# Attention decode, one core: keys loaded in rows of 64 KB instead of 32 KB, in a ring where two units overlap by half

## The chip, the cores and the metric

One core of one Trainium2 chip. Times are device microseconds (us) of that core, median of several executions. 1 KB is 1024 bytes where rows and loads are meant. A "packet" is what the trace records for one row of a load on one of the core's 16 transfer engines (DMA engines).

## The reference, cut to what matters

One token for each of 4 batches goes through attention over a cache of 8192 keys and values, and then through a gated layer. The caches are 256 MiB each in bf16, and each byte is used once.

```python
B, Sq, D = 4, 1, 512
H, Sk, Dh = 32, 8192, 128
q = (layernorm(x) @ wq).reshape(B, Sq, H, Dh).transpose(0, 2, 1, 3)
scores = einsum("bhqd,bhkd->bhqk", q, k_cache) * Dh ** -0.5
o = einsum("bhqk,bhkd->bhqd", softmax(scores), v_cache)
h = x + o.transpose(0, 2, 1, 3).reshape(B, Sq, H * Dh) @ wo
out = h + (sigmoid(ln(h) @ w_gate) * (ln(h) @ w_up)) @ w_down
```

## The kernel before

A *unit* is four heads of one batch: 8 MiB of keys and 8 MiB of values; there are 32. In SBUF a unit is 128 partitions of 64 KB, and partition p holds 256 consecutive positions of one head, so in memory too each partition's row is 64 KB in one piece.

A unit is worked off in 4 *steps* of 16 KB per partition. A step's keys are transposed by DVE (4 instructions), and PE computes their scores (16 matmuls). 8 steps, two units, make a *group*, after which comes one softmax. The values follow with 64 matmuls a unit ("PV").

The ring has four slots of 32 KB per partition. Values take a row of 64 KB (slots 2 and 3). Keys take two loads of 32 KB rows, one to slot 0, one to slot 1, and each slot is filled again as soon as its two steps are transposed.

```python
GS = 8            # steps in a group
NS = 4            # slots in the ring
LB = 16           # steps in a turn of the loops of PE and DVE
TW = R * 64       # elements of a slot: 32 KB per partition
HT = TW // 2      # elements of a step: 16 KB per partition
ring = SB("ring", [128, NS, TW], BF16)
kT = SB("kT", [128, 2, HT], BF16)              # transposed keys, two steps
bS, bO, bP = bank[0:2], bank[2:4], bank[4:6]   # PSUM: two score banks, two output banks

items = [("wq", 0)]
for u in range(NU):
    items += [("k", 2 * u), ("k", 2 * u + 1)]
    ...                                        # and the values of unit u - 1

# what a load waits for
prev_of[it] = [("k", it[1] - 2)]               # keys: the slot's last keys transposed
prev_of[it] = [("pv", it[1] - 1)]              # values: PV of the unit before
# ... [cut: first and last units]

def load(it):
    ...
    if kind == "k":
        dst, src = ringv(t % 2), kv_src(t // 2, A_k_cache)[:, (t % 2) * TW:(t % 2 + 1) * TW]
    elif kind == "v":
        dst, src = ringf[:, v_at(t, w0):...], kv_src(t, A_v_cache)[:, w0 * HT:w1 * HT]
    return [(lambda e: e.dma_start(dst, src).then_inc(sem, 16), sem, val)]

for s in range(NST):                           # 128 steps
    g, at = divmod(s, GS)
    dve_T(s)                                   # 4 transposes; wait for keys and for scores s - 2
    if s % 4 == 0 and s >= 8:
        pe_pv(s // 4 - 2, 0, 4)                # values of two units before
    pe_score(s)
    if at == GS - 1:
        ...                                    # softmax of the group
```

(Shortened; `...` marks cuts.) All loads but the 4 KB of x go through one queue (that of SyncE, "SPq"), in the order of `items`.

Of the kernel before, what the change touches and what calls it, by code (L numbers as in the profile page):

```python
# [14 lines left out]

GS = 8
NS = 4
LB = 16
# [12 lines left out]
class _Prog:  # L31

# [60 lines left out]
    def emit(self, name, e):  # L93
        seen = {}
        t0 = self.loops.get(name)
        done = False
        for op in self.ops[name]:
            if t0 is None or op.turn is None or op.turn < t0:
                self.put(name, e, op, op.deps, seen)
            elif not done:  # L100
                done = True
                self.emit_loop(name, e, t0, seen)

    def emit_loop(self, name, e, t0, seen):
        turns = {}
        for op in self.ops[name]:
            if op.turn is not None and op.turn >= t0:
                turns.setdefault(op.turn, {})[op.key] = op
        t1 = max(turns) + 1
# [55 lines left out]
def bass_sequential_preLN__mha_block_cached__glu_gated_glu__decode_kernel(  # L165
# [30 lines left out]
    prog = _Prog({"pe": 0, "dve": 0})  # L196
    P = prog.add

    with ExitStack() as es:
# [7 lines left out]
        kT = SB("kT", [128, 2, HT], BF16)  # L207
        LQ0 = 28
        Lq = SB("Lq", [128, NU * 16], BF16)
        Lqg = SB("Lqg", [128, 2, LQ0 + 260], BF16)  # L210
        ident = SB("ident", [128, 128], BF16)
        identf = SB("identf", [128, 128], FP32)
        onesf = SB("onesf", [128, 128], FP32)
# [39 lines left out]
        bS, bO, bP = bank[0:2], bank[2:4], bank[4:6]  # L253
# [11 lines left out]
        s_slot = [SEM(f"s_slot{i}") for i in range(3)]  # L265
# [8 lines left out]

        items = [("wq", 0)]
        for u in range(NU):
            items += [("k", 2 * u), ("k", 2 * u + 1)]
            if u == 0:
                items.append(("v", 0, 0, 1))
            elif u == 1:  # L280
                items.append(("v", 0, 1, 4))
            else:
                items.append(("v", u - 1, 0, 4))
        items += [("v", NU - 1, 0, 2), ("v", NU - 1, 2, 4)]
        items += [("wo", i) for i in range(NWO)] + [("wg", 0), ("wu", 0), ("wd", 0)]
        dma_of, prev_of = {}, {("v", 0, 0, 1): [("wq", 0)], ("v", 0, 1, 4): [("qr", 0)],
                               ("v", NU - 1, 0, 2): [("k", 2 * NU - 2)], ("v", NU - 1, 2, 4): [("k", 2 * NU - 1)]}
        for it in items:
            if it not in prev_of:
                if it[0] == "k":  # L290
                    prev_of[it] = [("k", it[1] - 2)] if it[1] >= 2 else []
                elif it[0] == "v":
                    prev_of[it] = [("pv", it[1] - 1)]
                elif it[0] in ("wg", "wu", "wd"):
                    prev_of[it] = [("pv", NU - 2)]
                else:
                    prev_of[it] = []
        consumed = {}

        wq_v = ring[:, 2, :].rearrange("p (c f) -> p c f", c=NDC)  # L300
        wo_v = kT[:, :, :].rearrange("p s f -> p (s f)").rearrange("p (s f) -> p s f", s=32)
        wg_v = ringv(2)[:, 0:NDC * F].rearrange("p (c f) -> p c f", c=NDC)
        wu_v = ringv(2)[:, NDC * F:2 * NDC * F].rearrange("p (c f) -> p c f", c=NDC)
        wd_v = ringv(3)[:, 0:NFT * D].rearrange("p (t f) -> p t f", t=NFT)
# [4 lines left out]

        def v_at(u, w):  # L310
            return (0 if u == NU - 1 else 2 * TW) + w * HT
# [5 lines left out]
        def load(it):  # L317
# [25 lines left out]
            if kind == "k":  # L343
                sem, val = s_slot[t % 2], 16 * (t // 2 + 1)
                dst, src = ringv(t % 2), kv_src(t // 2, A_k_cache)[:, (t % 2) * TW:(t % 2 + 1) * TW]
            elif kind == "v":
                w0, w1 = it[2:4]
                sem, val = (s_slot[2], 16 * (t + 2 if w1 == 4 else 1)) if t < NU - 1 else (s_slot[w0 // 2], 16 * (NU + 1))
                dst = ringf[:, v_at(t, w0):v_at(t, w0) + (w1 - w0) * HT]
                src = kv_src(t, A_v_cache)[:, w0 * HT:w1 * HT]  # L350
# [455 lines left out]
```

## Time and profile before

| | before |
|---|---|
| median time | 1283.74 us (1283.59 to 1283.95, 3 runs) |
| moved | 550.94 MB, mean 430 GB/s |
| share of the 16 engines' span taken by the loads' queue | 99.7% |
| DVE, PE, ACT busy | 51%, 40%, 6% |

The page of the kernel before. The first line gives the engines' busy time; DMA is the engines' mean busy share in 40 slices of the span, in tenths, and GB/s what they moved; the queue line gives packets, MB and share.

```profile
span 1281.9 us, 11257 instructions
## 1 busy us (share of the span) xinstructions
PE 509.5 (40%) x4755; PEld 191.7 (15%) x4755; DVE 657.3 (51%) x691; ACT 76.3 (6%) x150; POOL 5.6 (0%) x21
...
DMA  9999999999999999999999999999999999999998
GB/s 400 439 433 427 431 435 439 429 434 430 429 436 438 434 438 419 435 430 448 427 427 429 430 437 438 429 430 433 430 439 434 434 425 433 433 440 438 427 424 353
DMA packets 16117, 550.94 MB, mean 430 GB/s; under 512 B 1765, under 2 KB 1769, under 8 KB 3177
## 3 DMA queue, kind: packets, MB, share of 16 engines
q1 hardware_dynamic: 16096, 550.78, 99.7%
...
L494 DVE STREAM_TRANSPOSE kT<-ring 128x1024 uint32<-128x1024 uint32 x512 | 585.5, 1208 | 474.0 <-DMA ring<-in_A_k_cache_dram 474.0
L519 PE MATMUL PS<-kT,Lqg 128*32 128x512 bf16 x2048 | 242.9, 623 | 518.3 <-DVE kT L494 518.3
L541 PE MATMUL PS<-ring,PTz 128*32 128x512 bf16 x2048 | 184.9, 540 | 191.8 <-DMA ring<-in_A_v_cache_dram 184.8
...
ring<-in_A_k_cache_dram SPq DMA_DIRECT2D x64, 4096.0 KB, 29.5
```

How to read it: every compute engine is idle about half the time or more, and the groups say for whom: DVE waits for key loads (474.0 us), PE for DVE and value loads. The transfers hardly wait: they are at 9 (90% or more) in every slice but the last, and the loads' queue fills 99.7% of the span. The last line says that a key load lands 29.5 us after it is issued; it moves in 9.7 us (4 MiB at 430 GB/s), so it stood about 20 us in the queue. The queue is what must not run empty.

The chain of waits shows the same from the other end: load, transposes, next load. Columns: start us, us, what.

```profile
519.04 28.87 DMA ring<-in_A_k_cache_dram
547.91 0.02 issue
547.93 9.14 DVE kT L494 x8
557.07 0.02 issue
557.09 29.59 DMA ring<-in_A_k_cache_dram
```

72% of this chain is called DMA and 22% DVE, but the 9.14 us of transposes do not cost 9.14 us: while DVE works, other loads are in flight. A chain shows who released whom, not what a faster DVE would bring.

### The profile page before, as it was taken

The numbers are of one execution on the slowest core, as the hardware profiler recorded it, in microseconds if no ns is written. First come the engines' busy times: TensorE is split into PE (matmuls) and PEld (weight loads), VectorE is DVE, ScalarE is ACT, GpSimd is POOL, SyncE is SP. The second block draws the span as 40 slices with busy tenths as digits, with TensorE's granted clock in tenths as the row PEclk, the third lists the DMA queues.
The fourth block names the chain that finished last, engine by engine and source line by source line (L and its number), as shares of the span: only waits on it lengthen the run. The fifth ranks groups of instructions, "written<-read, shape, count | busy, mean of one in ns | idle before, by whom it ended". The sixth has DMA issues, their size and how long they took to land.

```text
span 1281.9 us, 11257 instructions
## 1 busy us (share of the span) xinstructions
PE 509.5 (40%) x4755; PEld 191.7 (15%) x4755; DVE 657.3 (51%) x691; ACT 76.3 (6%) x150; POOL 5.6 (0%) x21
## 2 busy tenths in 40 slices
PE   2343434343443343524344334343433435243345
PEld 0011101111111110201111111111101102011114
DVE  5763456634465543556534565443655435565330
ACT  2010100001010010100101000010100101001011
POOL 1000000000000000000000000000000000000000
PEclk9985556556556656555655555665566565556565
DMA  9999999999999999999999999999999999999998
GB/s 400 439 433 427 431 435 439 429 434 430 429 436 438 434 438 419 435 430 448 427 427 429 430 437 438 429 430 433 430 439 434 434 425 433 433 440 438 427 424 353
DMA packets 16117, 550.94 MB, mean 430 GB/s; under 512 B 1765, under 2 KB 1769, under 8 KB 3177
## 3 DMA queue, kind: packets, MB, share of 16 engines
q1 hardware_dynamic: 16096, 550.78, 99.7%
q8 instruction: 8, 0.13, 0.0%
q14 instruction: 5, 0.03, 0.0%
q10 hardware_dynamic: 8, 0.00, 0.0%
HBM read 550.77 MB, written 0.00 MB: 430 GB/s over the span
## 4 chain that ended last, share of the span: by engine, by line
DMA 72%; DVE 22%; PE 2%; SPq 2%; issue 2%; DVEq 0%; ACT 0%; ACTq 0%
DMA ring<-in_A_k_cache_dram 65%; DVE kT L494 21%; DMA ring<-in_A_v_cache_dram 5%; SPq L328 1%; PE PS L541 1%; DMA ring<-in_B_w_down_dram 1%; DMA ring<-in_A_wq_dram 1%; DVE Zs L615 1%; DVEq L158 0%; PE PS L426 0%; ACT PTz L609 0%; DVE ring L443 0%; PE PS L519 0%; DVE Lq L467 0%; SPq L339 0%
## 5 line engine op out<-in xcount | busy, mean ns | idle before, releaser
L494 DVE STREAM_TRANSPOSE kT<-ring 128x1024 uint32<-128x1024 uint32 x512 | 585.5, 1208 | 474.0 <-DMA ring<-in_A_k_cache_dram 474.0
L519 PE MATMUL PS<-kT,Lqg 128*32 128x512 bf16 x2048 | 242.9, 623 | 518.3 <-DVE kT L494 518.3
L541 PE MATMUL PS<-ring,PTz 128*32 128x512 bf16 x2048 | 184.9, 540 | 191.8 <-DMA ring<-in_A_v_cache_dram 184.8
L519 PEld LDWEIGHTS PS<-kT,Lqg 128*32 128x32 bf16 x2048 | 57.5, 126 | 672.3 <-DVE kT L494 460.5
L541 PEld LDWEIGHTS PS<-ring,PTz 128*32 128x32 bf16 x2048 | 69.0, 130 | 306.9 <-DMA ring<-in_A_v_cache_dram 174.2
L639 ACT ACTIVATE A_sb<-PS 32x32 bf16<-32x32 f32 x16 | 3.7, 230 | 929.5 <-PE PS L637 929.5
L599 DVE STREAM_TRANSPOSE Et<-Ep 128x512 bf16<-128x512 bf16 x16 | 11.4, 711 | 49.7 <-ACT Ep L594 49.7
L609 ACT ACTIVATE PTz<-Et 32x512 bf16<-32x512 bf16 x32 | 34.0, 1061 | 14.1 <-DVE Et L599 13.8
L623 PEld LDWEIGHTS PS<-SelZ,Zs 128*128 128x128 f32 x128 | 28.5, 328 | 14.3 <-issue 12.6
L623 PE MATMUL PS<-SelZ,Zs 128*128 128x8 f32 x128 | 30.0, 364 | 0.9 <-DVE Zs L615 0.9
L551 DVE TENSOR_REDUCE mx<-PS 128x1 f32<-128x512 f32 x16 | 11.1, 692 | 32.8 <-PE PS L519 32.8
L615 DVE TENSOR_SCALAR Zs<-PS,rinv 128x512 f32<-128x512 f32 x16 | 11.4, 712 | 24.3 <-PE PS L541 24.3
L610 DVE COPY PTz<-Et 32x512 bf16<-32x512 bf16 x32 | 18.8, 589 | 1.1
L590 PE MATMUL PS<-E_sb,Sel 128*32 128x512 bf16 x64 | 9.9, 608 | 17.4 <-ACT E_sb L574 17.4
L572 ACT ACTIVATE negm<-PS 128x1 f32<-128x1 f32 x16 | 2.7, 171 | 218.3 <-PE PS L568 218.3
L568 PE MATMUL PS<-onesf,rowx 1*128 1x1 f32 x32 | 9.3, 357 | 9.9 <-DVE rowx L563 9.9
L557 PE MATMUL PS<-identf,mx 128*1 128x128 f32 x16 | 6.0, 372 | 13.5 <-DVE mx L551 13.5
L574 ACT ACTIVATE E_sb<-PS,negm 128x512 bf16<-128x512 f32 x16 | 11.0, 687 | 0.8 <-ACT negm L572 0.3
L594 ACT ACTIVATE Ep<-PS 128x512 bf16<-128x512 f32 x16 | 9.6, 597 | 11.6 <-PE PS L590 11.6
L568 PEld LDWEIGHTS PS<-onesf,rowx 1*128 1x128 f32 x32 | 7.9, 306 | 14.6 <-DVE rowx L563 14.6
L579 PE MATMUL PS<-sig,Gsum 128*128 128x1 f32 x32 | 9.4, 363 | 0.0
L579 PEld LDWEIGHTS PS<-sig,Gsum 128*128 128x128 f32 x32 | 8.0, 313 | 7.0 <-issue 7.0
(86 smaller groups left out, 90.8 us busy)
## 6 DMA issues: line engine op xcount, KB each, us to landing
ring<-in_A_k_cache_dram SPq DMA_DIRECT2D x64, 4096.0 KB, 29.5
ring<-in_A_v_cache_dram SPq DMA_DIRECT2D x2, 4096.0 KB, 29.1
ring<-in_A_v_cache_dram SPq DMA_DIRECT2D x1, 6144.0 KB, 29.2
ring<-in_A_wq_dram SPq DMA_DIRECT2D x1, 4096.0 KB, 12.3
kT<-in_A_wo_dram SPq DMA_DIRECT2D x1, 2560.0 KB, 33.6
ring<-in_A_v_cache_dram SPq DMA_DIRECT2D x1, 2048.0 KB, 22.1
ring<-in_B_w_gate_dram SPq DMA_DIRECT2D x2, 896.0 KB, 26.5
ring<-in_B_w_up_dram SPq DMA_DIRECT2D x2, 896.0 KB, 30.0
```

The costliest lines, as they stand in the source:

```text
L328: return e.dma_start(wd_v[:, t0:t1, :], B_w_down.rearrange("(p t) f -> p t f", p=128)[:, t0:t1, :]).then_inc(s_piece[2 + i], 16)
L494: return e.transpose(kT[:, buf, i * q:(i + 1) * q].bitcast(U32), ringv(src)[:, base + i * q:base + (i + 1) * q].bitcast(U32))
L519: mm = e.matmul(bS[g % 2][32 * j:32 * (j + 1), :], Lqg[:, g % 2, l0:l0 + 32], rhs, start=(s % GS == 0 and v == 0), stop=(s % GS == GS - 1 ...
L541: mm = e.matmul(bO[g % 2][32 * rq:32 * (rq + 1), :], PTz[:, l0:l0 + 32], ringf[:, r0:r0 + 512], start=(i == 0 and w == 0 and j == 0), stop ...
L551: mx_of[g] = P("dve", lambda e: e.tensor_reduce(mx[:, :], bS[g % 2][:, :], AX.X, ALU.max), [sc_of[g * GS + GS - 1], p1_of.get(g - 1)], kin ...
L568: p2_of[g] = P("pe", lambda e: e.matmul(bX[:, 0:1], rowx[0:1, :], onesf[0:1, 0:1], start=True, stop=True), [d2b_of[g], c_ones], kind="p2")
L579: L_of[g] = P("pe", lambda e: e.matmul(bX[:, 0:1], Gsum[:, :], sig[:, 0:1], start=True, stop=True), [exp_of[g], a1_of[g], d_g], kind="L")
L599: et_of[g] = P("dve", lambda e: e.transpose(Et[:, :], Ep[:, :]), [epc_of[g]] + list(ptc_of.get(g - 1, ())), kind="et")
L609: return e.activation(dst, src, ACT.Copy)
L610: return e.tensor_copy(dst, src)
L615: z_of[g] = P("dve", lambda e: e.tensor_scalar(Zs[:, :], bO[g % 2][:, :], rinv[:, g % 2:g % 2 + 1], None, op0=ALU.mult), [pv_of[2 * g + 1] ...
L623: mm = e.matmul(bP[1][:, 0:8], Zs[:, 128 * r:128 * (r + 1)], SelZ[:, r, :], start=(r == 0), stop=(r == 3))
```

## The change

The intent: keys in rows of 64 KB too, so that half the packets go. A second full unit of keys beside the values would make the ring 192 KB per partition instead of 128; I took this not to fit. So keys get 96 KB (slots 0 to 2); even units lie at 0 to 64 KB, odd ones at 32 to 96. Two units in a row share the middle 32 KB, and each unit works off its shared half first, so the next unit's load can go after two of four steps. That is one slot more, 160 KB; other buffers give up room for it: transposed keys in three half-step buffers instead of two full steps, and PSUM and constants slimmed. PV comes a unit later, PTz copies go all to ACT, and the loop bodies are 8 steps long instead of 16. Cut to its core; two comments are added.

```diff
 GS = 8
-NS = 4
-LB = 16
+NS = 5
+LB = GS
...
-        kT = SB("kT", [128, 2, HT], BF16)
+        kT = SB("kT", [128, 3, HT // 2], BF16)
-        Lqg = SB("Lqg", [128, 2, LQ0 + 260], BF16)
+        Lqg = SB("Lqg", [128, LQ0 + 260], BF16)
...
-        bS, bO, bP = bank[0:2], bank[2:4], bank[4:6]
+        bS, bO, bP = bank[0:2], bank[2], bank[4:6]
...
+        def turned(u):
+            return (0, 1, 2, 3) if u % 2 else (2, 3, 0, 1)
         for u in range(NU):
-            items += [("k", 2 * u), ("k", 2 * u + 1)]
...
+            if u < 3:                                      # two loads of 32 KB rows
+                for w in turned(u)[0::2]:
+                    items.append(("k", u, w, w + 2))
...
             else:
-                items.append(("v", u - 1, 0, 4))
+                items += [("k", u, 0, 4), ("v", u - 2, 0, 4)]
...
+                    prev_of[it] = ("T", 4 * (u - 1) + 1)   # two steps of the unit before
...
+                    prev_of[it] = ("pv", min(u - 1, NU - 3))
...
+        def k_at(u, w):
+            return u % 2 * TW + w * HT
...
-                op = P("dve", f, [dma_of[it][0], sc_of.get(s - 2)], kind="T" if i == 3 else "Tpart")
+                op = P("dve", f, [dma_of[it][0], kT_last.get(buf) if i % 2 == 0 else None], ...)
...
+        def kT_buf(s, half):
+            return (2 * (s % LB) + half) % 3
...
-                    if a < 2:
-                        return e.activation(dst, src, ACT.Copy)
-                    return e.tensor_copy(dst, src)
+                    return e.activation(dst, src, ACT.Copy)
...  [cut: order of PV, softmax and output in the steps; first and last loads; where weights lie]
```

More of the change, by code (lines that the diff above doesn't have):

```diff
@@ L94, in emit @@
         seen = {}
-        t0 = self.loops.get(name)
+        t0, t1 = self.loops.get(name, (0, 0))
         done = False
         for op in self.ops[name]:
-            if t0 is None or op.turn is None or op.turn < t0:
+            if op.turn is None or not t0 <= op.turn < t1:
                 self.put(name, e, op, op.deps, seen)
@@ L101, in emit, with emit_loop @@
                 done = True
-                self.emit_loop(name, e, t0, seen)
-    def emit_loop(self, name, e, t0, seen):
+                self.emit_loop(name, e, t0, t1, seen)
+    def emit_loop(self, name, e, t0, t1, seen):
         turns = {}
         for op in self.ops[name]:
-            if op.turn is not None and op.turn >= t0:
+            if op.turn is not None and t0 <= op.turn < t1:
                 turns.setdefault(op.turn, {})[op.key] = op
-        t1 = max(turns) + 1
         mid = (t0 + t1) // 2
@@ L194, in bass_sequential_preLN__mha_block_cached__glu_gated_glu__decode_kernel @@
     EPS = 1e-5
-    prog = _Prog({"pe": 0, "dve": 0})
+    prog = _Prog({"pe": (0, NST // LB), "dve": (2, NST // LB)})
     P = prog.add
@@ L206, in bass_sequential_preLN__mha_block_cached__glu_gated_glu__decode_kernel @@
         ring = SB("ring", [128, NS, TW], BF16)
-        kT = SB("kT", [128, 2, HT], BF16)
+        kT = SB("kT", [128, 3, HT // 2], BF16)
         LQ0 = 28
         Lq = SB("Lq", [128, NU * 16], BF16)
-        Lqg = SB("Lqg", [128, 2, LQ0 + 260], BF16)
+        Lqg = SB("Lqg", [128, LQ0 + 260], BF16)
         ident = SB("ident", [128, 128], BF16)
         identf = SB("identf", [128, 128], FP32)
-        onesf = SB("onesf", [128, 128], FP32)
+        onesf = SB("onesf", [1, 1], FP32)
         meanf = SB("meanf", [128, 128], FP32)
@@ L264, in bass_sequential_preLN__mha_block_cached__glu_gated_glu__decode_kernel @@
         s_out = SEM("s_out")
-        s_slot = [SEM(f"s_slot{i}") for i in range(3)]
+        s_k, s_v = SEM("s_keys"), SEM("s_values")
+        s_half = [SEM(f"s_half{i}") for i in range(9)]
         s_piece = [SEM(f"s_piece{i}") for i in range(10)]
@@ L273, in bass_sequential_preLN__mha_block_cached__glu_gated_glu__decode_kernel @@
         NWO = len(WO_PARTS)
+        def turned(u):
+            return (0, 1, 2, 3) if u % 2 else (2, 3, 0, 1)
         items = [("wq", 0)]
         for u in range(NU):
-            items += [("k", 2 * u), ("k", 2 * u + 1)]
-            if u == 0:
-                items.append(("v", 0, 0, 1))
-            elif u == 1:
-                items.append(("v", 0, 1, 4))
-            else:
-                items.append(("v", u - 1, 0, 4))
-        items += [("v", NU - 1, 0, 2), ("v", NU - 1, 2, 4)]
+            if u < 3:
+                for w in turned(u)[0::2]:
+                    items.append(("k", u, w, w + 2))
+                    if (u, w) == (0, 0):
+                        items.append(("v", 0, 0, 1))
+                    elif (u, w) == (1, 2):
+                        items.append(("v", 0, 1, 2))
+                    elif (u, w) == (2, 0):
+                        items.append(("v", 0, 2, 4))
+            else:
+                items += [("k", u, 0, 4), ("v", u - 2, 0, 4)]
@@ L285, in bass_sequential_preLN__mha_block_cached__glu_gated_glu__decode_kernel @@
+        items += [("v", NU - 2, 0, 4), ("v", NU - 1, 0, 2), ("v", NU - 1, 2, 4)]
         items += [("wo", i) for i in range(NWO)] + [("wg", 0), ("wu", 0), ("wd", 0)]
-        dma_of, prev_of = {}, {("v", 0, 0, 1): [("wq", 0)], ("v", 0, 1, 4): [("qr", 0)],
-                               ("v", NU - 1, 0, 2): [("k", 2 * NU - 2)], ("v", NU - 1, 2, 4): [("k", 2 * NU - 1)]}
+        prev_of = {}
         for it in items:
-            if it not in prev_of:
-                if it[0] == "k":
-                    prev_of[it] = [("k", it[1] - 2)] if it[1] >= 2 else []
-                elif it[0] == "v":
-                    prev_of[it] = [("pv", it[1] - 1)]
-                elif it[0] in ("wg", "wu", "wd"):
-                    prev_of[it] = [("pv", NU - 2)]
-                else:
-                    prev_of[it] = []
@@ L298, in bass_sequential_preLN__mha_block_cached__glu_gated_glu__decode_kernel @@
-        consumed = {}
-        wq_v = ring[:, 2, :].rearrange("p (c f) -> p c f", c=NDC)
-        wo_v = kT[:, :, :].rearrange("p s f -> p (s f)").rearrange("p (s f) -> p s f", s=32)
-        wg_v = ringv(2)[:, 0:NDC * F].rearrange("p (c f) -> p c f", c=NDC)
-        wu_v = ringv(2)[:, NDC * F:2 * NDC * F].rearrange("p (c f) -> p c f", c=NDC)
-        wd_v = ringv(3)[:, 0:NFT * D].rearrange("p (t f) -> p t f", t=NFT)
+            kind, u = it[0:2]
+            if kind == "k":
+                if u < 3:
+                    prev_of[it] = {(1, 0): ("T", 1), (2, 2): ("T", 5), (2, 0): ("T", 3)}.get((u, it[2]))
+                else:
+                    prev_of[it] = ("T", 4 * (u - 1) + 1)
+            elif kind == "v":
+                if u == 0:
+                    prev_of[it] = ("wq", 0) if it[2] < 2 else ("qr", 0)
+                elif u == NU - 2:
+                    prev_of[it] = ("T", NST - 3)
+                else:
+                    prev_of[it] = ("pv", min(u - 1, NU - 3))
+            elif kind == "wo":
+                prev_of[it] = ("T", NST - 1)
+            elif kind != "wq":
+                prev_of[it] = ("pv", NU - 2)
@@ L306, in kv_src @@
+        dma_of = {}
+        consumed = {}
+        wq_v = ring[:, 3, :].rearrange("p (c f) -> p c f", c=NDC)
+        wo_v = ringv(2).rearrange("p (s f) -> p s f", s=32)
+        wg_v = ringv(0)[:, 0:NDC * F].rearrange("p (c f) -> p c f", c=NDC)
+        wu_v = ringv(0)[:, NDC * F:2 * NDC * F].rearrange("p (c f) -> p c f", c=NDC)
+        wd_v = ringv(1)[:, 0:NFT * D].rearrange("p (t f) -> p t f", t=NFT)
         def kv_src(u, cache):
@@ L308, in kv_src @@
             return cache[h // H, h % H:h % H + 4, :, :].rearrange("h (p r) d -> (h p) (r d)", p=32)
+        def k_at(u, w):
+            return u % 2 * TW + w * HT
         def v_at(u, w):
-            return (0 if u == NU - 1 else 2 * TW) + w * HT
+            return (0 if u == NU - 2 else 3 * TW) + w * HT
         ringf = ring[:, :, :].rearrange("p s f -> p (s f)")
@@ L342, in load @@
                 return ops
-            if kind == "k":
-                sem, val = s_slot[t % 2], 16 * (t // 2 + 1)
-                dst, src = ringv(t % 2), kv_src(t // 2, A_k_cache)[:, (t % 2) * TW:(t % 2 + 1) * TW]
-            elif kind == "v":
+            if kind in ("k", "v"):
                 w0, w1 = it[2:4]
-                sem, val = (s_slot[2], 16 * (t + 2 if w1 == 4 else 1)) if t < NU - 1 else (s_slot[w0 // 2], 16 * (NU + 1))
-                dst = ringf[:, v_at(t, w0):v_at(t, w0) + (w1 - w0) * HT]
-                src = kv_src(t, A_v_cache)[:, w0 * HT:w1 * HT]
+                at, cache = (k_at, A_k_cache) if kind == "k" else (v_at, A_v_cache)
+                dst = ringf[:, at(t, w0):at(t, w0) + (w1 - w0) * HT]
+                src = kv_src(t, cache)[:, w0 * HT:w1 * HT]
+                if kind == "k":
+                    sem, val = (s_half[2 * t + w0 // 2], 16) if t < 3 else (s_k, 16 * (t - 2))
+                elif t < NU - 2:
+                    sem, val = s_v, 16 * (t + 3) if t else 16 * min(w1, 3)
+                else:
+                    sem, val = s_half[6 + t - NU + 2 + w0 // 2], 16
             else:
@@ L372, in bass_sequential_preLN__mha_block_cached__glu_gated_glu__decode_kernel @@
         zlq = pool(lambda e: e.memset(Lq[:, :].bitcast(FP32), 0.0))
-        zlg = pool(lambda e: e.memset(Lqg[:, :, :].rearrange("p b f -> p (b f)").bitcast(FP32), 0.0))
+        zlg = pool(lambda e: e.memset(Lqg[:, :].bitcast(FP32), 0.0))
         zs = pool(lambda e: e.memset(Sel[:, :, :], 0.0))
@@ L385, in bass_sequential_preLN__mha_block_cached__glu_gated_glu__decode_kernel @@
         c_ones = pool(lambda e: e.memset(onesf[:, :], 1.0))
+        c_rinv = pool(lambda e: e.memset(rinv[:, :], 1.0))
         c_mean = pool(lambda e: e.memset(meanf[:, :], 1.0 / D))
@@ L480, in bass_sequential_preLN__mha_block_cached__glu_gated_glu__decode_kernel @@
                                                     AX.X, ALU.add), [c_selz4])
-        T_of, sc_of, pv_of, lqg_of = {}, {}, {}, {}
+        T_of, sc_of, pv_of, lqg_of, d3c_of = {}, {}, {}, {}, {}
         mx_of, d2_of, exp_of, pt_of, ptc_of, L_of, d3_of = {}, {}, {}, {}, {}, {}, {}
@@ L487, in dve_T @@
         def dve_T(s):
-            it = ("k", s // 2)
-            src, buf, base = it[1] % 2, s % 2, (s % 2) * HT
+            u = s // 4
+            w = turned(u)[s % 4]
+            it = next(it for it in items if it[0:2] == ("k", u) and it[2] <= w < it[3])
             q = HT // 4
@@ L492, in dve_T, with f @@
             for i in range(4):
-                def f(e, i=i):
-                    return e.transpose(kT[:, buf, i * q:(i + 1) * q].bitcast(U32),
-                                       ringv(src)[:, base + i * q:base + (i + 1) * q].bitcast(U32))
-                op = P("dve", f, [dma_of[it][0], sc_of.get(s - 2)], kind="T" if i == 3 else "Tpart")
-                yield
-            T_of[s] = op
-            consumed[it] = op
+                buf = kT_buf(s, i // 2)
+                def f(e, i=i, buf=buf):
+                    base = k_at(u, w) + i * q
+                    return e.transpose(kT[:, buf, i % 2 * q:(i % 2 + 1) * q].bitcast(U32), ringf[:, base:base + q].bitcast(U32))
+                op = P("dve", f, [dma_of[it][0], kT_last.get(buf) if i % 2 == 0 else None], kind="T" if i == 3 else "Tpart")
+            T_of[s] = consumed[("T", s)] = op
+        kT_last = {}
+        def kT_buf(s, half):
+            return (2 * (s % LB) + half) % 3
         def chain_lq(g):
             lqg_of[g] = P("act", lambda e: e.activation(
-                Lqg[:, g % 2, LQ0:LQ0 + 256].rearrange("p (i a) -> p i a", a=32)[:, :, 0:4],
+                Lqg[:, LQ0:LQ0 + 256].rearrange("p (i a) -> p i a", a=32)[:, :, 0:4],
                 Lq[:, 32 * g:32 * g + 32].rearrange("p (i a) -> p i a", a=4), ACT.Copy),
-                [sc_of.get((g - 2) * GS + GS - 1), zlg] + ([o for ops in lq_of for o in ops] if g == 0 else []), kind="lq")
+                [sc_of.get(g * GS - 1), zlg] + ([o for ops in lq_of for o in ops] if g == 0 else []), kind="lq")
         def pe_score(s):
-            u, w, i, g = s % 2, s % 4, s // 4 % 2, s // GS
+            u, g = s // 4, s // GS
+            w, i = turned(u)[s % 4], u % 2
             hh = 2 * w + i
@@ L516, in f @@
                     for j in range(4):
-                        rhs = bass.AP(kT, u * HT + j * (HT // 4) + 64 * (v // 2) + (v % 2),
-                                      [[2 * HT, 128], [128, 16], [2, 32]])
-                        mm = e.matmul(bS[g % 2][32 * j:32 * (j + 1), :], Lqg[:, g % 2, l0:l0 + 32], rhs,
+                        k0 = kT_buf(s, j // 2) * (HT // 2) + j % 2 * (HT // 4) + 64 * (v // 2) + v % 2
+                        rhs = bass.AP(kT, k0, [[3 * HT // 2, 128], [128, 16], [2, 32]])
+                        mm = e.matmul(bS[0][32 * j:32 * (j + 1), :], Lqg[:, l0:l0 + 32], rhs,
                                       start=(s % GS == 0 and v == 0), stop=(s % GS == GS - 1 and v == 3),
@@ L524, in pe_score @@
             if s % GS == 0:
-                deps += [exp_of.get(g - 2), lqg_of[g]]
+                deps += [exp_of.get(g - 1), lqg_of[g]]
             if s == 0:
                 deps += q_ev
-            sc_of[s] = P("pe", f, deps, kind="sc")
+            kT_last[kT_buf(s, 0)] = kT_last[kT_buf(s, 1)] = sc_of[s] = P("pe", f, deps, kind="sc")
         def pe_pv(u, w0, w1):
@@ L540, in f @@
                             r0 = v_at(u, w) + (16 * j + 4 * rq) * 128
-                            mm = e.matmul(bO[g % 2][32 * rq:32 * (rq + 1), :], PTz[:, l0:l0 + 32], ringf[:, r0:r0 + 512],
+                            mm = e.matmul(bO[32 * rq:32 * (rq + 1), :], PTz[:, l0:l0 + 32], ringf[:, r0:r0 + 512],
                                           start=(i == 0 and w == 0 and j == 0), stop=(i == 1 and w == 3 and j == 3),
@@ L546, in pe_pv @@
             if i == 0:
-                deps.append(z_of.get(g - 2))
+                deps.append(z_of.get(g - 1))
             pv_of[u] = consumed[("pv", u)] = P("pe", f, deps, kind="pv")
         def chain_mx(g):
-            mx_of[g] = P("dve", lambda e: e.tensor_reduce(mx[:, :], bS[g % 2][:, :], AX.X, ALU.max),
+            mx_of[g] = P("dve", lambda e: e.tensor_reduce(mx[:, :], bS[0][:, :], AX.X, ALU.max),
                          [sc_of[g * GS + GS - 1], p1_of.get(g - 1)], kind="mx")
@@ L573, in chain_exp @@
                          [p2_of[g], exp_of.get(g - 1)], kind="a1")
-            exp_of[g] = P("act", lambda e: e.activation(E_sb[:, :], bS[g % 2][:, :], ACT.Exp, bias=negm[:, 0:1],
+            exp_of[g] = P("act", lambda e: e.activation(E_sb[:, :], bS[0][:, :], ACT.Exp, bias=negm[:, 0:1],
                                                         scale=SCALE, accum_out=sig[:, 0:1]),
@@ L582, in chain_d3, with chain_d3c @@
         def chain_d3(g):
-            d3_of[g] = P("dve", lambda e: e.reciprocal(rinv[:, g % 2:g % 2 + 1], bX[:, 0:1]), [L_of[g], z_of.get(g - 2)], kind="d3")
+            d3_of[g] = P("dve", lambda e: e.reciprocal(rinv[:, 0:1], bX[:, 0:1]), [L_of[g], d3c_of.get(g), c_rinv], kind="d3")
+        def chain_d3c(g):
+            d3c_of[g] = P("dve", lambda e: e.tensor_copy(rinv[:, 1:2], rinv[:, 0:1]), [d3_of.get(g - 1), z_of.get(g - 2), c_rinv],
+                          kind="d3c")
         def chain_pt(g):
@@ L607, in fc @@
                     src = Et[p0:p0 + 32, :].rearrange("p (q r m) -> p q m r", q=4, r=4)
-                    if a < 2:
-                        return e.activation(dst, src, ACT.Copy)
-                    return e.tensor_copy(dst, src)
-                ops.append(P("act" if a < 2 else "dve", fc, [et_of[g], zp] + last_pv, kind="ptc" if a < 2 else "ptd"))
+                    return e.activation(dst, src, ACT.Copy)
+                ops.append(P("act", fc, [et_of[g], zp] + last_pv, kind="ptc"))
             ptc_of[g] = ops
         def chain_z(g):
-            z_of[g] = P("dve", lambda e: e.tensor_scalar(Zs[:, :], bO[g % 2][:, :], rinv[:, g % 2:g % 2 + 1], None,
-                                                         op0=ALU.mult), [pv_of[2 * g + 1], d3_of[g], ot_of.get(g - 1)],
+            z_of[g] = P("dve", lambda e: e.tensor_scalar(Zs[:, :], bO[:, :], rinv[:, 1:2], None,
+                                                         op0=ALU.mult), [pv_of[2 * g + 1], d3c_of[g + 1], ot_of.get(g - 1)],
                         kind="z")
@@ L648, in bass_sequential_preLN__mha_block_cached__glu_gated_glu__decode_kernel @@
                 chain_lq(g)
-            for _ in dve_T(s):
-                pass
-            if s % 4 == 0 and s >= 8:
-                pe_pv(s // 4 - 2, 0, 4)
-            if g >= 1 and at == 4:
-                chain_z(g - 1)
-            if g >= 1 and at == 5:
-                chain_otc(g - 1)
+            dve_T(s)
+            if at == 0 and g >= 2:
+                pe_pv(2 * g - 3, 0, 4)
+                chain_z(g - 2)
+            if at == 1 and g >= 2:
+                chain_otc(g - 2)
+            if at == 1 and g >= 1:
+                chain_et(g - 1)
+            if at == 4 and g >= 1:
+                pe_pv(2 * g - 2, 0, 4)
             pe_score(s)
-            if g >= 1 and at == 4:
-                chain_ot(g - 1)
-            if g >= 1 and at == 5:
-                chain_a(g - 1)
+            if at == 0 and g >= 2:
+                chain_ot(g - 2)
+            if at == 1 and g >= 2:
+                chain_a(g - 2)
             if at == GS - 1:
@@ L669, in bass_sequential_preLN__mha_block_cached__glu_gated_glu__decode_kernel @@
                 chain_L(g)
-                chain_et(g)
+                chain_d3c(g)
                 chain_d3(g)
         prog.step = None
+        pe_pv(NU - 3, 0, 4)
+        chain_z(NG - 2)
+        chain_et(NG - 1)
+        chain_ot(NG - 2)
+        chain_otc(NG - 2)
+        chain_a(NG - 2)
+        chain_d3c(NG)
         pe_pv(NU - 2, 0, 4)
@@ L754, in bass_sequential_preLN__mha_block_cached__glu_gated_glu__decode_kernel @@
             for op in dma_of[it]:
-                op.deps = [sc_of[NST - 1]] if it[0] == "wo" else [consumed[p] for p in prev_of[it]]
+                op.deps = [consumed[prev_of[it]]] if prev_of.get(it) else []
         prog.resolve(sem_of)
```

## The prediction

> **What bounds the kernel now.** The transfers. The DMA page gives 550.94 MB at a mean of 430 GB/s, and one queue fills 99.7% of the 16 engines' span. Every one of the 40 slices but the last shows DMA at 9, while DVE is 51%, PE 40% and ACT 6% busy (page, part 1). The packet records add up to 1278.5 us per engine, within 1 us of the first-to-last packet time (1279.4 us). So only the transfers' own cost, or an empty queue, can move the time. [...]
>
> **What the change removes.** A row of a load is one packet. A 32 KB packet takes 1218.5 ns in the mean, a 64 KB one 2422.1 ns: two short ones cost 2437.1, so 15.0 ns go per packet saved. Keys are 8192 packets of 32 KB; after, units 3 to 31 make 3712 packets of 64 KB and units 0 to 2 stay at 768 of 32 KB. 3712 packets fewer x 15.0 ns / 16 engines = 3.48 us. Unit 0's values come in three pieces instead of two: 128 packets more, -0.12 us. There are 28 loads fewer, each of which posts a 4-byte packet of 9 ns per engine: 0.25 us. Sum 3.6 us, 0.28%, all on the critical path. 1283.7 - 3.6 = 1280.1 us.
>
> **What it adds.** Tighter refilling. Say a key unit lands at t; a unit transfers in 19.4 us.
> - Next key unit: needs two steps' transposes (9.14 us per 8, chain of waits), issued at about t+11; the values in flight end at t+19.4. Spare about 5 us, after 2.1 us of spread between first and last engine and 1 us from issue to first packet.
> - Values: on every second unit the PV matmuls (5.2 to 5.9 us) now stand behind the softmax chain. Estimate: 16 transposes 18.3, score 1.9, chain to the row sums 5.0, PV 5.9: issued at about t+32, needed by t+35.7. Spare 3 to 4 us.
> - Start: key unit 2's first load waits for transposes that end 1 to 2 us before the queue would run dry. A bubble of 0 to 2 us, once.
> - Three half-step key buffers: a step's second half needs the last score done: 1.9 us of score against 2.3 us of first-half transposes. It just fits.
> - One score and one output bank instead of two, PTz copies all on ACT (4 x 1.06 us), an 8-step loop: off the critical path.
>
> **Prediction.** 1280.1 us; 8 in 10 between 1278.8 and 1283.0. Faster by over 2%: 0.00 (2% is 25.7 us; the packet overhead of all keys is 8 us). Within 2%: 0.97. Slower by over 2%: 0.03.
>
> **What would show it.** Packets 16117 to about 12,400; mean 64 KB packet still about 2422 ns; DMA share still 99% or more; mean about 431 GB/s; DVE waits on key DMA still the longest; PE and DVE busy nearly unchanged.
>
> **What would make it wrong.** An empty queue: if a refill misses its slot by 1 us every second unit, 15 us come on top (1295 us), the DMA share falls below 99% and the DMA queue's own waits on PE or DVE end at that moment. Or 64 KB key packets slower than value packets.

## The result, and the profile after

| | before | after |
|---|---|---|
| median time | 1283.65 us (1283.59 to 1283.95, 6 runs) | 1281.56 us (1281.34 to 1281.83, 6 runs) |
| packets | 16117 | 12084 |
| mean record of a 64 KB packet, 100 to 1180 us | 2422.1 ns | 2421.9 ns |
| mean record of a 32 KB packet, 100 to 1180 us | 1217.2 ns | none |
| one unit of values landing after the last, steady part | 38.78 us | 38.70 us |
| last load landed | 1278.82 us | 1276.62 us |

The ratio is 0.9983 (95% interval 0.9970 to 0.9996). Ratios are the mean time of one kernel's fast runs over that of the other's of the same rounds, so not quite the ratio of the medians. The kernel is 2.1 us faster, where 3.6 us were predicted.

The page of the kernel after, the same lines.

```profile
span 1279.7 us, 11348 instructions
## 1 busy us (share of the span) xinstructions
PE 484.7 (38%) x4755; PEld 187.1 (15%) x4755; DVE 636.3 (50%) x676; ACT 109.2 (9%) x182; POOL 5.3 (0%) x22
...
DMA  9999999999999999999999999999999999999998
...
DMA packets 12084, 550.93 MB, mean 431 GB/s; under 512 B 1316, under 2 KB 1320, under 8 KB 2728
## 3 DMA queue, kind: packets, MB, share of 16 engines
q1 hardware_dynamic: 12064, 550.77, 99.7%
...
L523 DVE STREAM_TRANSPOSE kT<-ring 128x1024 uint32<-128x1024 uint32 x512 | 583.4, 1206 | 488.5 <-DMA ring<-in_A_k_cache_dram 488.5
L551 PE MATMUL PS<-kT,Lqg 128*32 128x512 bf16 x2048 | 242.8, 623 | 713.5 <-DVE kT L523 713.5
L573 PE MATMUL PS<-ring,PTz 128*32 128x512 bf16 x2048 | 165.9, 495 | 17.7 <-DMA ring<-in_A_v_cache_dram 17.7
...
ring<-in_A_k_cache_dram SPq DMA_DIRECT2D x29, 28.8
```

DMA is at 9 in the same 39 slices and the queue's share is the same 99.7%. PV no longer waits for value loads (17.7 us of idle time instead of 184.8), PE waits for DVE instead, and ACT took the PTz copies. None of this shows in the time, as the transfers set it and not the compute engines.

What did change in kind is how long a load stands in the queue. For each load the trace tells when it was issued and when the first engine reported that it had finished the load before it; the difference I call the *spare time*, within which the new load must reach the engines.

| spare time, us, loads issued after 80 us | before | after |
|---|---|---|
| key loads | 17.0 to 17.9 | 7.2 to 8.4 |
| value loads up to 1200 us | 6.0 (the first), then 10.6 to 12.3 | 5.9 to 11.4 |

The spare time of keys was halved, but it is nowhere near zero. The chain of waits after, where a key load is now 8 MiB (19.4 us of transfer) and lands 28.78 or 29.52 us after issue:

```profile
544.67 2.34 DVE kT L523 x2
547.01 0.02 issue
547.02 28.78 DMA ring<-in_A_k_cache_dram
...
582.63 2.34 DVE kT L523 x2
584.97 0.02 issue
584.98 29.52 DMA ring<-in_A_k_cache_dram
```

**Where the predicted 3.6 us went, from the two traces.** The sum used 15.0 ns per packet saved: two records of 1218.5 ns against one of 2422.1. Both halves of that were inflated.

- The mean of 1218.5 ns includes the first packets of the run: 15 of them, begun within 2.2 us of the span's start, took 1553 to 2267 ns. From 100 us on the mean is 1217.2. That takes 2.6 ns off a pair.
- Records of consecutive packets on an engine overlap. From 100 to 1180 us the trace before has 16.039 packets open at a time on 16 engines; the surplus, divided by all packets, is 3.5 ns a packet (after: the same). A record is thus 3.5 ns longer than the time that the packet adds, and removing a packet frees 3.5 ns less than its record says.

So 2 x (1217.2 - 3.5) - (2422.1 - 3.5) = 8.8 ns a packet (an estimate: 8.4 if the surplus is laid on the data packets alone, 9.0 if only the loads' queue is counted). The sum again: 3712 x 8.8 / 16 = 2.04 us, less 128 x 8.8 / 16 = 0.07, plus 28 x (9 - 3.5) ns = 0.15: 2.1 us, as measured. This fits, but so might a loss in refills. Experiments had to tell.

### The profile page after: what moved, and what is told of

It is laid out like the page before. It is cut to its first block, busy times and chain, and to the rows that moved or that the text cites. A ratio compares the mean times of both kernels' runs of the same rounds, so it can differ in the third digit from the quotient of the medians.

```text
span 1279.7 us, 11348 instructions
## 1 busy us (share of the span) xinstructions
PE 484.7 (38%) x4755; PEld 187.1 (15%) x4755; DVE 636.3 (50%) x676; ACT 109.2 (9%) x182; POOL 5.3 (0%) x22
## 2 busy tenths in 40 slices
DMA packets 12084, 550.93 MB, mean 431 GB/s; under 512 B 1316, under 2 KB 1320, under 8 KB 2728
## 3 DMA queue, kind: packets, MB, share of 16 engines
q1 hardware_dynamic: 12064, 550.77, 99.7%
HBM read 550.77 MB, written 0.00 MB: 430 GB/s over the span
## 4 chain that ended last, share of the span: by engine, by line
DMA 72%; DVE 21%; issue 3%; SPq 2%; PE 1%; DVEq 0%; ACT 0%
DMA ring<-in_A_k_cache_dram 68%; DVE kT L523 20%; DMA ring<-in_A_v_cache_dram 2%; DMA ring<-in_B_w_down_dram 1%; DMA ring<-in_A_wq_dram 1%; SPq L360 1%; SPq L349 1%; DVE Zs L649 1%; PE PS L573 0%; PE PS L451 0%; DVEq L158 0%; PE PS L551 0%; DVE ring L468 0%; DVE Lq L492 0%; PE PS L781 0%
## 5 line engine op out<-in xcount | busy, mean ns | idle before, releaser
L573 PE MATMUL PS<-ring,PTz 128*32 128x512 bf16 x2048 | 165.9, 495 | 17.7 <-DMA ring<-in_A_v_cache_dram 17.7
L644 ACT ACTIVATE PTz<-Et 32x512 bf16<-32x512 bf16 x64 | 68.8, 1076 | 358.4 <-DVE Et L635 357.2
L573 PEld LDWEIGHTS PS<-ring,PTz 128*32 128x32 bf16 x2048 | 65.5, 123 | 113.1 <-issue 76.5
L649 DVE TENSOR_SCALAR Zs<-PS,rinv 128x512 f32<-128x512 f32 x16 | 11.4, 714 | 34.9 <-PE PS L573 34.9
L615 DVE RECIPROCAL rinv<-PS 128x1 f32<-128x1 f32 x16 | 2.7, 168 | 45.3 <-PE PS L611 45.3
L593 DVE TENSOR_REDUCE mrow<-PS 1x8 f32<-1x128 f32 x16 | 4.5, 279 | 7.4 <-PE PS L589 7.4
```

Of the source, the lines that this page charges most:

```text
L573: mm = e.matmul(bO[32 * rq:32 * (rq + 1), :], PTz[:, l0:l0 + 32], ringf[:, r0:r0 + 512], start=(i == 0 and w == 0 and j == 0), stop=(i == ...
L644: return e.activation(dst, src, ACT.Copy)
L649: z_of[g] = P("dve", lambda e: e.tensor_scalar(Zs[:, :], bO[:, :], rinv[:, 1:2], None, op0=ALU.mult), [pv_of[2 * g + 1], d3c_of[g + 1], ot ...
```

## The experiments

**Theory A**: a packet costs some 9 ns in itself, the change saved packets and nothing else, and the new ring costs nothing because the queue never runs empty. **Rival B**: a packet costs the predicted 15 ns, and the new ring gives 1.5 us back in late refills. **Rival C**: what counts is the number of loads, not of packets.

Loops that wait on a value in a register could not be run in experiments. So all of them have the loops of PE and DVE written out in full, and two controls show what that alone does.

### Controls: both kernels with their loops written out

```diff
-    prog = _Prog({"pe": (0, NST // LB), "dve": (2, NST // LB)})
+    prog = _Prog({})
```

u_before (its own loop line is `_Prog({"pe": 0, "dve": 0})`). Expected:

> Control: the kernel before, its PE and DVE loops written out in full (no other edit), since loops that wait on register values are not to be run in experiments. Both theories: within 3 us of the kernel before (1283.65 us); what it costs is the fetching of more instruction bytes by the same transfer engines. Key and value loads should never find the queue empty (least spare time at issue about 10 us).

Measured: 1289.85 us (1289.82 to 1290.02), 6.3 us over the looped one. That is more than the 3 us allowed: a miss for both theories. The least spare time of a load from 80 to 1200 us was 6.4 us, where about 10 was expected.

u_after. Expected:

> Control: the changed kernel, its loops written out. Both theories: 2.1 us (2.0 to 2.3) under u_before, as the looped pair differ, and one unit of keys and values every 38.70 us against 38.78 in u_before. If the 8-step loop bodies themselves had helped or hurt, the difference would be another one.

Measured: 1287.48 us (1287.41 to 1287.62), 2.37 us under u_before. That is 0.3 us more than the looped pair and just above the stated range, so the loop bodies themselves had little to do with the gain.

Both are slower than with loops, by 5.9 and 6.3 us. The page of u_after shows more fetched instructions among the packets of the transfer engines (queue 8: 37 packets, where the looped kernel has 7):

```profile
DMA packets 12118, 551.46 MB, mean 429 GB/s; under 512 B 1316, under 2 KB 1320, under 8 KB 2728
## 3 DMA queue, kind: packets, MB, share of 16 engines
q1 hardware_dynamic: 12064, 550.77, 99.3%
q8 instruction: 37, 0.61, 0.2%
```

Each is 16 KB and takes 1.07 us of an engine's time, and the 64 KB packet right behind it on that engine takes 2.9 us instead of 2.42: 1.57 us in all. (The looped kernels' traces have the same: 8 and 7 such packets of 1.06 and 1.08 us in the mean, and a 64 KB packet of 2.90, 2.97 or 2.89 us as one ends.) The packet records do not name the engine, but they let it be inferred who pays. The fetches' durations repeat every eighth time, and late in the run seven of the 16 engines still finish a load within 1 us of each other while the other nine come 5 us or more later: so it seems, though no run tested it, that these fetches go round eight engines (the ninth would be the one with the 8 KB fetches of another queue, see pool_pad), and that the rest carry none. 30 fetches more on eight engines are 30 / 8 x 1.57 = 5.9 us on each of them (an estimate from these records), as much as the written-out loops cost. The spread between the first and the last engine to finish a load grows from 1.9 us to 6.9 us through the run, and the spare time falls from 8 us to 3 for keys and to 1.3 for one value load. So the controls are good baselines, but with less spare time late in the run than the looped kernel has.

### k32_two_loads: the new ring with the old packets

```diff
+        s_k2 = SEM("s_keys2")
+            if kind == "k" and t >= 3:
+                h = TW
+                return [(lambda e: e.dma_start(dst[:, 0:h], src[:, 0:h]).then_inc(s_k, 16), s_k, val),
+                        (lambda e: e.dma_start(dst[:, h:2 * h], src[:, h:2 * h]).then_inc(s_k2, 16), s_k2, val)]
-                op = P("dve", f, [dma_of[it][0], kT_last.get(buf) if i % 2 == 0 else None], ...)
+                op = P("dve", f, dma_of[it] + [kT_last.get(buf) if i % 2 == 0 else None], ...)
```

> u_after with each 64 KB key load (units 3 to 31) cut into two loads of 32 KB rows, both issued at the same moment as the one load was, transposes waiting for both; ring, overlap, buffers and order stay. Theory A (packet count is all that the change bought): about 2.1 to 2.2 us over u_after, so level with u_before within 0.4 us, 38.78 us a unit. Rival B (the new ring and refill cost or win time by themselves, packets give the predicted 3.5 us of which 1.5 are lost in refills): 3.5 us over u_after, 1.4 us slower than u_before.

Measured: 1289.64 us (1289.58 to 1289.84), 2.16 us over u_after and 0.2 us under u_before. In the median a unit lands 38.78 us after the last, as expected, against 38.70 in u_after and 38.81 in u_before. The whole gain goes when the rows are cut, and no more than the gain. The ring, the overlap, the half-step buffers, the single output bank, ACT's copies: together they are worth 0.2 to 0.3 us (k32_two_loads has 128 value packets more than u_before, about 0.07 us). Rival B asked for 3.5 us and a time above u_before; it is out.

### k32_one_load: one load, two packets a row

Lest two runs that touch be merged into one packet (that they would be is not shown), they are walked in reverse order; the data land in the same places.

```diff
+            if kind in ('k',) and dst.shape[1] == 2 * TW:
+                def turned_rows(a):
+                    s = a.rearrange("p (n f) -> p n f", n=2)
+                    ap = [list(x) for x in s.ap]
+                    ap[1][0] = -ap[1][0]
+                    return bass.AP(s.tensor, s.offset + 2 * TW - 2 * TW // 2, ap)
+                return [(lambda e: e.dma_start(turned_rows(dst), turned_rows(src)).then_inc(sem, 16), sem, val)]
```

> u_after with each 64 KB key load left one load, but walked as two runs of 32 KB in reverse order, so that a row is two packets (the data land where they did). Tells packets from loads. Theory A, packets: 8.7 ns x 8 packets a unit, 2.0 us over u_after, and k32_two_loads a further 0.15 us over it (one more completion packet a unit). Rival C, the number of loads: level with u_after. Should the packet count not rise (runs merged), the run tells nothing.

Measured: 1289.58 us (1289.45 to 1289.80), 2.10 us over u_after with the same number of loads. The packets rose as intended, from 12118 to 15830 (its page's line, to be set against that of u_after), which is 232 an engine: 2.10 us / 232 = 9.1 ns a packet.

```profile
DMA packets 15830, 551.46 MB, mean 428 GB/s; under 512 B 1316, under 2 KB 1320, under 8 KB 2728
```

The second load of k32_two_loads adds 0.06 us more (0.15 expected), which is within the scatter. Rival C is out.

### kv16 and kv8: more packets still

The edit of k32_one_load for keys and values both, with n=4 (kv16) and n=8 (kv8).

> u_after with every 64 KB row of keys (units 3 to 31) and values (units 1 to 30) still in one load but walked as four runs of 16 KB in reverse order: 59 loads x 8 rows an engine x 3 packets more = 1416 packets more an engine. If a packet costs a constant 8.7 ns (what the 32 KB rows cost in steady state): 12.3 us over u_after. If it costs the 15.0 ns of the prediction: 21 us. If it costs what the 16 KB records at the start of the traces say (611 ns, less 3.5 of overlap: 11.5 ns for a whole row of 64 KB): 5.4 us.

> The same with eight runs of 8 KB: 3304 packets more an engine. Constant 8.7 ns: 28.7 us over u_after. 15.0 ns: 50 us. By the few 8 KB records of the traces (308 ns, less 3.5: 17.5 ns a row): 8.3 us.

Measured: kv16 1300.66 us (1300.56 to 1300.84), 13.2 us over u_after; kv8 1318.30 us (1317.97 to 1318.39), 30.8 us over. These ran on another chip; the kernel before, run beside both, was within 0.1 us (1283.58 and 1283.66).

| run | packets more per engine | us over u_after | ns per packet |
|---|---|---|---|
| k32_one_load | 232 | 2.10 | 9.1 |
| kv16 | 1416 | 13.18 | 9.3 |
| kv8 | 3304 | 30.82 | 9.3 |

One constant from 64 KB down to 8 KB. The 15.0 ns of the prediction would have given 21 and 50 us. The third guess, from the few 16 and 8 KB records at hand, is wrong as well: kv16's own steady 16 KB packets take 615.8 ns in the mean where the early ones of the kernel before took 611. Packets that run in an unusual moment, or few of them, mislead in both directions.

The median records of the kernel before (3.5, 32 and 64 KB), of kv16 and of kv8 lie on one line: 12 ns plus the bytes at 27.19 bytes/ns (fit to 3.5, 8, 16, 32 and 64 KB: 142, 314, 615, 1218, 2422 ns, all within 2 ns). 12 ns less the 3.5 of overlap is 8.5 ns. The slope times 16 engines is 435.0 GB/s.

### hold3, hold4 and hold_half: how much lateness does the ring bear?

In the kernel after, a key load waits for two steps of the unit before. hold3 makes it three steps, hold4 all four (which takes the overlap's use away), hold_half two and a half.

```diff
-                    prev_of[it] = ("T", 4 * (u - 1) + 1)
+                    prev_of[it] = ("T", 4 * (u - 1) + 2)      # hold3; hold4: + 3; hold_half: second of that step's transposes
```

> u_after with key units 3 to 31 let go one step later (after three steps' transposes of the unit before instead of two), 4.6 us later. In u_after a key load is issued 3.2 to 8.5 us before the first engine runs dry and about 10 us before the last one does; issue to first packet is 1 us. Theory A (transfers set the time, the slowest engine's backlog counts): within 0.5 us of u_after, though the first engine does run dry late in the run. Rival B (refills are already losing time): each microsecond of delay shows, 29 units x up to 4.6 us, tens of us.

Measured: 1296.62 us (1292.27 to 1297.16, more scatter than any other run), 9.1 us over u_after. This was a miss: I expected no cost.

> u_after with key units 3 to 31 let go only when the whole unit before is transposed, 9.2 us later: the half overlap of the two units is undone in effect. Theory A: now a unit takes 4 steps' transposes (19.2 us), 1 us to the first packet, 19.35 us of transfer and about 0.5 us to land and start, 40.0 us instead of 38.8: 30 to 45 us over u_after (1317 to 1333 us), with the queue empty about 1 us a unit. If the overlap were of no use: level with u_after.

Measured: 1370.43 us (1367.61 to 1371.79), 83 us over u_after. Right in kind, and far over the 30 to 45 us expected. (Of its terms, the traces of the two looped kernels show that an engine reports its share of a load as finished 0.46 us, in the median, after the end of its 4-byte packet; for the time to the first packet see below.) The chain of waits of hold4:

```profile
510.67 21.74 DMA ring<-in_A_k_cache_dram
532.40 0.02 issue
532.43 18.16 DVE kT L523 x16
550.58 0.02 issue
550.60 24.06 DMA ring<-in_A_k_cache_dram
...
594.20 21.90 DMA ring<-in_A_k_cache_dram
616.10 0.02 issue
616.12 18.15 DVE kT L523 x16
634.28 0.02 issue
634.29 22.93 DMA ring<-in_A_k_cache_dram
```

Now load and transposes do follow each other without anything else in flight, and a unit takes 41.9 us (532.40 to 616.10 is two). The queue's share fell (the queue line of its page):

```profile
q1 hardware_dynamic: 12064, 550.77, 94.6%
```

The packet records say why it was 3 us a unit and not 1.2. The first packet comes 0.95 us after the start of the issuing instruction (which takes 0.33 us), but where the queue had run dry the sixteenth engine has its first only after 1.6 to 2.0 us, and the first packet on each engine then mostly takes 2.7 to 3.5 us instead of 2.42. Over the 25 units looked at, an engine was idle for 2.3 us and its packets 0.65 us too long in the mean, each time: 3.0 us x 29 units = 87 us, near the 83 measured.

In hold3 the same happens in part. Units whose load had 2.7 us of spare time or more lost little or nothing; those between 0.5 and 2.3 us lost 0.1 to 1.2 us each in idle and slow packets, and after the first held unit alone the kernel was 2.2 us behind u_after. So in this run a refill needed some 2.5 us of spare time, and not the 1 us from issue to first packet that I had put in. From this came one more run:

> u_after with key units 3 to 31 let go half a step later (after two and a half steps' transposes), about 2.4 us later. hold3 (4.6 us later) cost 9.1 us where no cost was expected; its trace lays the cost on the units whose load was issued under about 2.5 us before the first engine ran dry. Theory A' (a refill costs only under that spare of about 2.5 us): key loads keep 5 to 6 us of spare in the first third, cost nothing there, and cost 0.2 to 0.4 us each only in the last units, where the spare of u_after (3.2 to 4.5 us) falls under 2.5: 1 to 4 us in all over u_after, from the last third. Rival D (the hold itself slows every unit alike): half of hold3's 9.1 us, 0.15 us a unit from the first held unit on.

Measured: 1287.59 us (1287.30 to 1287.81), 0.1 us over u_after: no cost at all, neither the 1 to 4 us of theory A' nor the 4.5 of rival D. The spare time of its key loads was 4.4 us or more in the first 360 us and 1.8 to 4.3 later. Late in a run with written-out loops the last engine is 5 to 7 us behind the first, so when the first engine runs dry the one that sets the time still has work; in hold3, the dear units came early, when all engines ran dry nearly together. The trace of hold_half agrees: the load issued at 708 us finds seven engines within 1.8 us of running dry, and their first packets take 3.1 to 4.1 us; the other nine have 4.0 us or more left, and this unit's last engine is done 38.6 us after the last unit's, so not late. That reading fits both runs, but no run was made to test it: where exactly the limit lies stays open. What is shown is that half a step more (2.4 us) is free, a whole step (4.6 us) is not, and two steps cost 83 us.

### pool_pad: are fetched instructions what the written-out loops cost?

```diff
+        scr = SB("scr", [128, 2304], mybir.dt.uint8)
+        last = c_mean
+        for turn in range(3):
+            for n in range(2304):
+                op = P("pool", lambda e, n=n: e.memset(scr[0:1, n:n + 1], 0.0), [last] if n == 0 else [],
+                       kind="padlast" if n == 2303 else "pad")
+            last = op
```

> u_after with 6912 one-byte clears of a scratch row on the idle POOL engine, nobody waiting for them: more instructions to fetch, no work in anyone's way. Written-out loops cost 5.9 to 6.3 us against looped ones; the trace has 37 fetch packets of 16 KB against 7, and the spread between the first and the last engine to finish a load grows from 1.9 to 6.9 us through the run. Theory F (fetches take transfer time on one engine after another and the most burdened engine sets the end): some 27 more fetch packets, 4 to 6 us over u_after, more (up to 10) where the fetches make the spare of refills vanish. Rival (the written-out loops cost time because PE and DVE wait for instructions): within 0.5 us of u_after.

Measured: 1318.10 us (1317.72 to 1318.59), 30.6 us over u_after, five times what I expected. The page:

```profile
POOL 8777777771000000000000000000000000000000
...
DMA  9999998999999999999999999999999999999997
GB/s 401 408 431 414 384 382 364 406 384 385 413 419 419 434 425 435 431 434 431 434 429 432 435 432 432 434 429 440 429 431 438 425 438 432 427 442 424 436 421 324
...
q1 hardware_dynamic: 12064, 550.77, 97.6%
q8 instruction: 37, 0.61, 0.2%
q14 instruction: 63, 0.52, 0.1%
```

DVE and PE were as busy as in u_after (636.4 and 488.2 us), and nobody waits for POOL. Yet the rate drops while POOL runs through its 6912 instructions, and only then: at 340 us the kernel is 34 us behind u_after, and it falls no further behind afterwards. 54 more fetch packets of 8 KB came in 300 us, the spread between engines rose to 15 us, and the spare time of refills fell below zero (-2.9 us). So instructions that nobody waits for slow this kernel; the rival is out for this run.

The packet records say how. From 110 to 290 us, 15 of the engines finish each load within about 2 us of each other, and one comes 12 to 15 us behind. Followed packet by packet, each starting as the one before it ends, this one engine carries 43 of the 44 fetches of this queue between 60 and 300 us: 0.32 us each in the mean, and the 64 KB packet right behind one takes 2.77 us instead of 2.42. (In the looped kernels' traces three such fetches of 0.31 us have 64 KB packets of 2.80 to 2.83 us behind them.) Its other packets take their usual 2.42 us, so it is the fetches that cost, and not what the clears write. 54 x 0.67 us = 36 us if it bears them all (an estimate), against 34 us by which it is behind. The other 15 wait for it, because a refill waits for the whole load; their negative spare time is a consequence, and hardly anything is left for it to add. So theory F had the kind of cost right, but not its size: these fetches did not go round all engines, and each cost double its own record (0.67 us against 0.32).

## Why the prediction was right or wrong

By its range and its class it was right: 1281.56 us lies between 1278.8 and 1283.0, and the change is within 2%. Its middle, a gain of 3.6 us, was 1.7 times the measured gain. It also put the need of a refill too low, but the spare time that it foresaw (4 us or more before its 1 us is taken off) covers the 2.5 us that hold3 showed as well, so this did no harm.

- **The bound: right.** Transfers before and after, 99.7% of the engines' span both times. PE's and DVE's own work is off the path: k32_two_loads has all of the new structure and the old packets, and is level with u_before to 0.2 us.
- **The mechanism: right.** The gain is the packets saved. Cutting rows in two takes it all back (2.10 and 2.16 us) with one load or two.
- **The size: 3.6 us predicted, 2.1 measured.** The term that was mis-sized is "15.0 ns go per packet saved". The experiments give 9.1 to 9.3 ns; records overlap by 3.5 ns each, and the mean of 32 KB packets held the slow ones of the start.
- **"Packets 16117 to about 12,400": 12,084.** I forgot to take the completion packets of 28 loads, 448, out of the count.
- **Spare time: right in kind.** Predicted, net of 1 us to the first packet: 5 us for keys, 3 to 4 for values. Measured less that 1 us: 6.2 to 7.4 and at least 4.9. But the need of 1 us was too small: hold3 cost 9.1 us with half a microsecond to almost 4 left. The looped kernel has 5.9 us at its tightest load.
- **Start: no bubble seen.** Key unit 2's first load was issued 3.6 us before the first engine ran dry, and the kernel after was ahead by 0.2 to 0.3 us at the loads of the start that compare.
- **"PE and DVE busy nearly unchanged": less right.** DVE lost 21 us (copies that went to ACT), PE 25 us, 19 of them in PV matmuls (495 ns in the mean instead of 540; single ones took 378 to 635 ns in both traces, and the median went from 631 to 380; the cause was not shown). It cost and gained nothing: k32_two_loads has these too.

No version here beats the kernel after. Every experiment has written-out loops, which cost 6 us. By the fitted line what remains is small: 550.77 MB at 435.0 GB/s would take 1266 us, and 12064 packets x 8.5 ns / 16 are 6.4 us (an estimate); the rest is start and end.

## What to carry to other kernels

To cost a change of packet size, take records from the steady part only, subtract what consecutive records overlap (3.5 ns each here), and check that the corrected records add up to the span; a difference of two large records is at the mercy of a few ns in each. When a change leaves a saturated queue saturated, compute for each load the spare time between its issue and the moment the queue would run dry, before and after: it is the margin that the change spends (for keys from 17.0 to 17.9 us down to 7.2 to 8.4), and the share of busy time does not show it (99.7% both times). And in this kernel, bound by transfers, fetched instructions were transfers too: in pool_pad one engine, to which 43 of 44 fetches were traced, fell 12 to 15 us behind in its loads and held up the others, and the loops were worth more (5.9 us) than the row sizes (2.1 us).
